# Longformer attention with an FFN: weight decode moved from the prelude into the first FFN group

## The chip, the cores and the metric

The kernel runs on one core of one Trainium2 chip. The metric is device time in microseconds (us) of one execution. Before the change it is 1021.1 us, the median of 3 runs (1018.6 to 1021.68).

## What is computed

The inputs are queries, keys and values of 8 batches x 8 heads: 512 local tokens and 32 global ones, 64 wide. Local tokens attend to the global ones and to local ones within 32 positions; global tokens attend to all. The result goes through a feed-forward network (FFN) with weights of 512 x 2048 and 2048 x 512. All of it is float32.

```python
def _attn_ref(q_l, k_l, v_l, q_g, k_g, v_g):
    ...
    s_g = scale * np.matmul(q_g, k_all.transpose(0, 1, 3, 2))
    out_g = np.matmul(sm(s_g), v_all)
    s_ll = scale * np.matmul(q_l, k_l.transpose(0, 1, 3, 2))
    mask = np.abs(pos[:, None] - pos[None, :]) <= window
    s_ll = np.where(mask, s_ll, -1000000000.0)
    ...
    out_l = np.matmul(a_l, np.concatenate([v_g, v_l], axis=2))

def _moe_ref(x, w_in, w_out, alpha):
    h = x @ w_in
    g = np.maximum(h, 0.0) + alpha * np.minimum(h, 0.0)
    return (g @ w_out).astype(np.float32)
```

The weights reach the kernel as the bits of float64 numbers, so it has to decode them into float32 before it can use them.

## The kernel before

**Units.** The main loop counts t from -19 (NPRE is 19); u = t + 19 is the unit. Units 0 to 18 are the *prelude*: attention only, because the FFN needs the attention of a whole batch first. From unit 19 on, every unit also does one step of the FFN.

**Attention** goes by pairs of heads: 32 pairs P, four to a batch, four units to a pair (unit 4P + s). In a unit, `local_scores` takes a quarter of a pair's scores (PE), adds the mask (VectorE, L243) and exponentiates (ScalarE, L247); `softmax_tail` normalizes (L208, L209, L214). Once per pair, `global_softmax` starts with a row maximum on VectorE (L270), in unit 4P + 2; it serves below as a mark of how far attention has come. The transposes and the product with the values of pair P come in units 4P + 2 to 4P + 6.

**FFN** goes by groups: eight groups of 512 local tokens (one batch each), and one of 256 global tokens. A group has 16 steps f, one per unit. `f1` multiplies the attention's result, split in two float32r halves `xh` and `xl` by `split_x` (L386, L387), with the f-th block of w_in, 12 matmuls into `h_ps`; VectorE applies the activation (L404, L405), ScalarE and GpSimd split the result into `gh` (L407) and `gl` (L408). `f2`, two units later (LAG), adds 12 matmuls into the group's outputs `o`. So the first group is units 19 to 34, and L404 marks the units in the trace. The next group can start when the four pairs of its batch are through.

**Weight decode.** The weights are 32 pieces of 512 KB, piece 2f of w_in and 2f + 1 of w_out. A piece is loaded on SP's queue (`load_weights`, L104). `decode_words` takes two ScalarE operations (L112, L113), three of VectorE (L114, L116, L117) and an add on GpSimd (L119). One unit later `split_weights` takes one of ScalarE (L125) and a subtraction on GpSimd (L126). After that the piece stays in SBUF for the rest of the kernel. f1 of step f needs piece 2f, from unit 19 + f on; f2 needs piece 2f + 1, from unit 21 + f on.

**What sets the order.** `weights_step(u)` stands at the end of each unit. RATE says how many pieces it decodes: the first tuple, by u modulo its length, in the prelude, the second from unit 19 on. With `((1, 1, 0), (2, 1))` the prelude's units decode 13 pieces, and units 19 to 31 the other 19: two in even units, one in odd ones. Each decode of piece i also issues the load of piece i + 6; the first six loads are issued ahead of the loop, right behind the first load of queries and keys (`load_pair(0)`).

The order within each engine's queue is made when the program is built: a planner goes by program order as priority and by a simulated time, so that work whose inputs are there may be put ahead of earlier work that waits. From unit 4 on the attention has a priority of 50 places ahead (HP, HPU). From unit 36 (PIN) PE's matmuls keep program order. Working tiles share pools: the tag "st" has 18 buffers (NST), for `xh`, `xl`, `g`, `gh`, `gl`, the values `vx`, and the `t` and `r` of decode; the tag "w" has 33 (NWB), for raw and for decoded weights.

In units 0 to 17 `keep_warm` adds four matmuls on zeros to each unit.

Of the kernel before, what the change touches and what calls it, by code (L numbers as in the profile page):

```python
# [44 lines left out]
GS = (2, "mid")  # L45
EV = dict(pt0=(2, "mid"), pt1=(4, "pre"), ptg=(4, "pre"), pv0=(5, "mid"), pv1=(6, "mid"))
SM = (2, "post")
RATE = ((1, 1, 0), (2, 1))
GROUPS = [("l", b) for b in range(NB)] + [("g", 0)]


# [8 lines left out]
def longformer_ffn(ctx: ExitStack, tc: tile.TileContext, qk, qkr, gn, vt, vx, w, alpha, out):  # L60
# [41 lines left out]
    def load_weights(f, j):  # L102
        wraw[f, j] = wpool.tile([128, 1024], U32, tag="w", name="wraw")
        nc.sync.dma_start(wraw[f, j], w[f, j].bitcast(U32))  # L104
# [3 lines left out]
    def decode_words(f, j):  # L108
        words = wraw.pop((f, j)).rearrange("p (n two) -> p n two", two=2)
        low, high = words[:, :, 0], words[:, :, 1]  # L110
        t, r = stage("wt"), stage("wr", I32)
        nc.scalar.activation(t, high.bitcast(F32), AF.Abs)  # L112
        nc.scalar.activation(r, low, AF.Copy, scale=2.0**-29)  # L113
        nc.vector.tensor_scalar(t, t, CLAMP_LO, CLAMP_HI, op0=ALU.max, op1=ALU.min)  # L114
        tu = t.bitcast(U32)
        nc.vector.tensor_scalar(tu, tu, 3, 0x3FFFFFFF, op0=ALU.logical_shift_left, op1=ALU.bitwise_and)  # L116
        nc.vector.scalar_tensor_tensor(tu, high, 0xC0000000, tu, op0=ALU.bitwise_and, op1=ALU.bitwise_or)  # L117
        ti = t.bitcast(I32)
        nc.gpsimd.tensor_tensor(ti, ti, r, op=ALU.add)  # L119
        wmid[f, j] = t  # L120

    def split_weights(f, j):
        t = wmid.pop((f, j))
        wt = wpool.tile([128, 2, 512], F32R, tag="w", name="wt")
        nc.scalar.copy(wt[:, 0, :], t)  # L125
        nc.gpsimd.tensor_tensor(wt[:, 1, :], t, wt[:, 0, :].bitcast(F32), op=ALU.subtract)  # L126
        wts[f, j] = wt
# [50 lines left out]
    def load_pair(P):  # L178
        hi[P] = work.tile([128, NQ + NKR], F32, tag="hi", name="qk_raw", bufs=2)
        nc.sync.dma_start(hi[P], qkr[P])  # L180
# [348 lines left out]
    pieces = [(f, j) for f in range(NF) for j in range(2)]  # L529
    ahead = 6  # L530
    state = [0]

    def weights_step(u):
        k = state[0]
        n = RATE[0][u % len(RATE[0])] if u < NPRE else RATE[1][u % len(RATE[1])]
        new = [i for i in range(k, min(k + n, len(pieces)))]
        for i in new:
            if i + ahead < len(pieces):
                load_weights(*pieces[i + ahead])
            decode_words(*pieces[i])  # L540
        state[0] += len(new)
        done.append([pieces[i] for i in new])
        if len(done) > 1:
            for key in done.pop(0):
                split_weights(*key)
# [4 lines left out]
        return tc.high_priority(offset=HP) if u >= HPU else nullcontext()  # L550

    load_pair(0)
    for k in range(ahead):
        load_weights(*pieces[k])
    NT = len(GROUPS) * NF
    for t in range(-NPRE, NT + LAG):
        u = t + NPRE
        pinned[0] = u >= PIN
        if u < NWARM:
            keep_warm(WARM[0])  # L560
        with boost(u):
            attn_pre(u)
        G, f = divmod(t + 1, NF)
        last = 0 <= t + 1 < NT and f == 0
        if 0 <= t < NT:
            f1(t)
        if last:
            for c in range(NC - 1):
                split_x(G, c)
        with boost(u):  # L570
            attn_mid(u)
        if last:
            split_x(G, NC - 1)
        if t >= LAG:
            f2(t - LAG, 0)
        if u < NWARM:
            keep_warm(WARM[1])
        with boost(u):
            attn_post(u)
        if t >= LAG:  # L580
            f2(t - LAG, 1)
        weights_step(u)
# [74 lines left out]
```

## Time and profile before

| | |
|---|---|
| median of 3 runs | 1021.1 us |
| the profiled execution | 1017.19 us, its span 1015.4 us |
| PE busy | 984.7 us, 97% of the span |
| VectorE (DVE) busy | 659.9 us, 65% |
| ScalarE (ACT) busy | 507.4 us, 50% |
| GpSimd (POOL) busy | 407.7 us, 40% |
| DMA | 133.01 MB, 131 GB/s on the mean |
| first L404 (start of the FFN) | 95.96 us |
| L404 of the second group's first step | 231.69 us |
| last add of a decode (L119) | 201.58 us |

The profile is of one execution; times in it count from the start of its span. An instruction has a line of the kernel, an engine, the tile that it writes and those that it reads. Matmuls are pipelined, so a PE that is shown busy need not be at its peak. A row in square brackets after an instruction tells how long its engine was idle before it, and what it waited for. The chain of waits is followed back from the last instruction: at each step to what released it.

### The profile page before, as it was taken

The numbers are of one execution on the slowest core, as the hardware profiler recorded it, in microseconds if no ns is written. First come the engines' busy times: TensorE is split into PE (matmuls) and PEld (weight loads), VectorE is DVE, ScalarE is ACT, GpSimd is POOL, SyncE is SP. The second block draws the span as 40 slices with busy tenths as digits, with TensorE's granted clock in tenths as the row PEclk, the third lists the DMA queues.
The fourth block names the chain that finished last, engine by engine and source line by source line (L and its number), as shares of the span: only waits on it lengthen the run. The fifth ranks groups of instructions, "written<-read, shape, count | busy, mean of one in ns | idle before, by whom it ended". The sixth has DMA issues, their size and how long they took to land.

```text
span 1015.4 us, 17227 instructions
## 1 busy us (share of the span) xinstructions
PE 984.7 (97%) x5592; PEld 790.2 (78%) x5592; DVE 659.9 (65%) x2274; ACT 507.4 (50%) x1347; POOL 407.7 (40%) x330
## 2 busy tenths in 40 slices
PE   7798989998999999999999999999999999999998
PEld 4455767776888888888888888888888888888798
DVE  8978778776666766676767666766667665322322
ACT  6667566575445555455446555654555542211121
POOL 7611567653344344334344344433443432222222
PEclk9987999999999999999999999999999999999999
DMA  9545432145444554455455554455455532100010
GB/s 349 224 141 176 140 116 68 60 123 185 147 138 133 177 158 137 141 167 169 135 152 158 171 153 143 144 179 157 118 149 178 159 107 79 42 1 1 1 43 22
DMA packets 95275, 133.01 MB, mean 131 GB/s; under 512 B 10192, under 2 KB 53712, under 8 KB 95184
## 3 DMA queue, kind: packets, MB, share of 16 engines
q1 hardware_dynamic: 95184, 131.91, 41.5%
q8 instruction: 44, 0.72, 0.3%
q14 instruction: 47, 0.39, 0.1%
HBM read 100.93 MB, written 30.93 MB: 130 GB/s over the span
## 4 chain that ended last, share of the span: by engine, by line
PE 84%; DVE 9%; ACT 2%; issue 2%; DMA 1%; POOL 0%; SPq 0%; DVEq 0%; ACTq 0%; POOLq 0%
PE o L92 35%; PE h_ps L92 35%; PE o_ps L92 5%; PE s_ps L92 5%; PE g_ps L92 3%; DVE wt L114 1%; DVE wt L117 1%; DVE pt_sb L318 1%; DVE p_sb L243 1%; PE warm L92 1%; ACT p_sb L214 1%; DVE g L404 1%; DVE wt L116 1%; DVE g L405 1%; ACT p_sb L247 0%
## 5 line engine op out<-in xcount | busy, mean ns | idle before, releaser
L92 PE MATMUL h_ps<-xh,wt 128*128 128x512 f32 (+1 forms) x1152 | 351.8, 389 | 2.8 <-DVE g L405 2.8
L408 POOL TENSOR_TENSOR gl<-g,gh 128x512 fp32r<-128x512 f32 (+1 forms) x144 | 177.5, 1233 | 418.1 <-ACT gh L407 382.6
L92 PE MATMUL o<-gh,wt 128*128 128x512 f32 (+1 forms) x1152 | 282.5, 386 | 1.5 <-ACT ost L302 1.5
L92 PEld LDWEIGHTS o<-gh,wt 128*128 128x128 f32 x1152 | 205.8, 188 | 48.5 <-ACT ost L302 2.5
L92 PEld LDWEIGHTS h_ps<-xh,wt 128*128 128x128 f32 x1152 | 207.4, 191 | 43.4 <-DVE g L405 3.3
L92 PE MATMUL h_ps<-xl,wt 128*128 128x512 f32 (+1 forms) x576 | 222.4, 387 | 0.9 <-DVE xl L387 0.9
L407 ACT CAST gh<-g 128x512 fp32r<-128x512 f32 (+1 forms) x144 | 86.1, 598 | 260.9 <-DVE g L405 241.4
L404 DVE TENSOR_SCALAR g<-h_ps,alpha_sb 128x512 f32<-128x512 f32 (+1 forms) x144 | 103.3, 717 | 125.3 <-PE h_ps L92 123.0
L214 ACT ACTIVATE p_sb<-p_sb,rz 128x192 f32<-128x192 f32 (+1 forms) x252 | 102.3, 454 | 118.1 <-DVE rz L209 115.8
L92 PE MATMUL o<-gl,wt 128*128 128x512 f32 (+1 forms) x576 | 151.4, 383 | 0.0
L247 ACT ACTIVATE p_sb<-p_sb,mn 128x224 f32<-128x224 f32 (+2 forms) x256 | 115.8, 454 | 39.5 <-DVE mn L243 39.3
L92 PEld LDWEIGHTS h_ps<-xl,wt 128*128 128x128 f32 x576 | 109.4, 190 | 25.2 <-DVE xl L387 1.1
L92 PEld LDWEIGHTS o<-gl,wt 128*128 128x128 f32 x576 | 104.5, 188 | 23.9 <-issue 0.8
L208 DVE TENSOR_SCALAR rz<-z 128x1 f32<-128x1 f32 x256 | 38.3, 151 | 97.4 <-ACT p_sb L247 96.0
L297 DVE STREAM_TRANSPOSE pt_sb<-sg_sb 32x64 f32<-32x64 f32 x384 | 90.6, 236 | 10.6 <-ACT sg_sb L280 4.9
L192 POOL TENSOR_TENSOR hi<-rawq,hi 64x512 fp32r<-64x512 f32 x48 | 62.1, 1294 | 88.0 <-DMA vt<-in_vt_dram 50.1
L405 DVE SCALAR_TENSOR_TENSOR g<-h_ps,g 128x512 f32<-128x512 f32 (+1 forms) x144 | 94.1, 653 | 2.8
L195 POOL TENSOR_TENSOR kl<-rawk,hi 128x640 fp32r<-128x640 f32 x48 | 75.9, 1582 | 3.8
L119 POOL TENSOR_TENSOR wt<-wt,wr 128x512 int32<-128x512 int32 x32 | 42.4, 1324 | 77.2 <-DVE rz L208 40.2
L243 DVE CUSTOM_DVE_ANT_0 p_sb<-s_ps,mask 128x192 f32<-128x192 f32 x192 | 64.3, 364 | 13.5 <-PE s_ps L92 11.9
L92 PE MATMUL o_ps<-pt_sb,vt 128*64 128x160 f32 (+4 forms) x832 | 68.2, 288 | 3.6 <-ACT pt_sb L302 1.7
L92 PEld LDWEIGHTS o_ps<-pt_sb,vt 128*64 128x64 f32 (+2 forms) x832 | 48.7, 135 | 21.9 <-issue 11.9
(85 smaller groups left out, 1043.7 us busy)
## 6 DMA issues: line engine op xcount, KB each, us to landing
scratch<-p_sb SPq DMA_DIRECT2D x192, 112.0 KB, 2.4
wraw<-in_w_dram SPq DMA_DIRECT2D x32, 512.0 KB, 6.7
vt<-in_vt_dram SPq DMA_DIRECT2D x32, 512.0 KB, 4.9
rawk<-in_qk_dram SPq DMA_DIRECT2D x96, 160.0 KB, 2.9
rawq<-in_qk_dram SPq DMA_DIRECT2D x96, 128.0 KB, 2.7
pt_sb<-scratch SPq DMA_DIRECT2D x48, 256.0 KB, 2.8
gn<-in_gn_dram SPq DMA_DIRECT2D x32, 304.0 KB, 5.3
pt_sb<-scratch SPq DMA_DIRECT2D x48, 192.0 KB, 2.9
```

The costliest lines, as they stand in the source:

```text
L92: ins = nc.tensor.matmul(*a, **k)
L119: nc.gpsimd.tensor_tensor(ti, ti, r, op=ALU.add)
L192: nc.gpsimd.tensor_tensor(q, raw[64:128], q.bitcast(F32), op=ALU.subtract)
L195: nc.gpsimd.tensor_tensor(kl[P, h], raw, t.bitcast(F32), op=ALU.subtract)
L214: nc.scalar.activation(r, r, AF.Copy, scale=rz[:parts, e : e + 1])
L243: nc.vector.tensor_tensor_reduce(out=pr, in0=s[:, 256 * e : 256 * e + nn], in1=masks[e], scale=-0.125, scalar=3.0e38, op0=ALU.add, op1=ALU ...
L247: nc.scalar.activation(pr, pr, AF.Exp, bias=mn[:, e : e + 1], scale=-1.0, accum_out=z[:, e : e + 1])
L297: nc.vector.transpose(dst, src)
L404: nc.vector.tensor_scalar(g[:, 0:n], h[:, 0:n], 0.0, alpha_sb[:, f : f + 1], op0=ALU.min, op1=ALU.mult)
L405: nc.vector.scalar_tensor_tensor(g[:, 0:n], h[:, 0:n], 0.0, g[:, 0:n], op0=ALU.max, op1=ALU.add)
L407: nc.scalar.copy(gh[:, 0:n], g[:, 0:n])
L408: nc.gpsimd.tensor_tensor(gl[:, 0:n], g[:, 0:n], gh[:, 0:n].bitcast(F32), op=ALU.subtract)
```

## The change

RATE becomes `((0, 0, 1), (2,))`. In the prelude one piece is decoded in every third unit (2, 5, 8, 11, 14, 17): six pieces in place of 13. Units 19 to 31 decode two pieces each: 26 in place of 19. In both kernels the last piece is in unit 31. The first six loads are no longer issued ahead of the loop, but one at the end of each of the units 0 to 5, behind the attention's loads of these units.

```diff
-RATE = ((1, 1, 0), (2, 1))
+RATE = ((0, 0, 1), (2,))
...
     def weights_step(u):
+        if u < ahead:
+            load_weights(*pieces[u])
         k = state[0]
...
     load_pair(0)
-    for k in range(ahead):
-        load_weights(*pieces[k])
     NT = len(GROUPS) * NF
```

## The prediction

> **What bounds the kernel now.** I read the windows view first, cut where the kernel changes its work: 20 to 60 us (attention with weight decode), 60 to 86 us (attention alone), 104 to 200 us (first FFN group, attention and decode), and 200 to 232 us (the end of that group). Columns: stretch, length, then busy time of PE, PEld, DVE, ACT and POOL.
>
> ```profile
> 20.00:60.00 40.00, 32.41 (x171) 20.17 (x170) 34.29 (x105) 24.70 (x68) 26.23 (x20) 0.87 0.63 239
> 60.00:86.00 26.00, 24.39 (x241) 15.63 (x239) 20.63 (x117) 20.53 (x72) 0.00 (x0) 1.00 0.39 124
> 104.00:200.00 96.00, 91.73 (x547) 68.67 (x548) 77.20 (x207) 59.92 (x145) 62.01 (x48) 0.96 0.30 101
> 200.00:232.00 32.00, 30.82 (x176) 24.36 (x175) 24.23 (x93) 20.35 (x56) 15.68 (x13) 0.95 0.38 111
> ```
>
> Two things are to be seen. GpSimd does nothing at all from 60 to 86 us, so decode sits in two blocks with a hole between them: one early in the prelude, one in the first FFN group. And in the second block no engine has much to spare: PE 91.7 of 96 us, VectorE 77.2, GpSimd 62.0. Next I read the chain of waits (start, length, what), to see which of them leads.
>
> ```profile
> 95.96 0.75 DVE g L404
> ...
> 97.49 5.49 PE h_ps L92 x12
> ...
> 110.98 1.55 DVE wt L117
> 112.62 1.28 POOL wt L119
> 113.92 0.70 ACT wt L112
> ...
> 192.20 2.80 PE h_ps L92 x12
> ```
>
> Around 110 us the chain walks through one piece of decode on three engines (L117, L119, L112); at 192 us it is plain matmuls. So the first FFN group is bound by decode in its first part and by PE in its last. The FFN starts at 95.96 us (unit 19, the first L404).
>
> **What the prelude gains.** Of 13 pieces in the prelude's units, 6 stay. What a piece costs there is read from the spacing of the pairs, by the row maximum L270, once per pair (pairs 0, 1, 2 and 4):
>
> ```profile
> 20.77 0.44 DVE L270 TENSOR_REDUCE gm<-g_ps 128x1 f32<-128x288 f32 x1
> 40.88 0.45 DVE L270 TENSOR_REDUCE gm<-g_ps 128x1 f32<-128x288 f32 x1
> 59.64 0.46 DVE L270 TENSOR_REDUCE gm<-g_ps 128x1 f32<-128x288 f32 x1 [1.48 <-PE g_ps L92]
> 86.12 0.46 DVE L270 TENSOR_REDUCE gm<-g_ps 128x1 f32<-128x288 f32 x1 [0.82 <-PE g_ps L92]
> ```
>
> From pair 0 to pair 2 take 38.9 us, with eight pieces of decode among them; from pair 2 to pair 4 take 26.5 us with none. A piece costs the prelude (38.9 - 26.5) / 8 = 1.55 us. When are they decoded?
>
> ```profile
> 43.77 0.67 ACT L112 ACTIVATE wt<-wraw 128x512 f32<-128x512 f32 x1
> ...
> 88.96 0.62 ACT L386 CAST xh<-x_raw 128x512 fp32r<-128x512 f32 x1
> 89.96 0.68 ACT L112 ACTIVATE wt<-wraw 128x512 f32<-128x512 f32 x1
> ...
> 97.47 0.62 ACT L407 CAST gh<-g 128x512 fp32r<-128x512 f32 x1 [1.11 <-DVE g L405]
> 97.99 0.68 ACT L112 ACTIVATE wt<-wraw 128x512 f32<-128x512 f32 x1
> ```
>
> L112 opens a piece. The twelfth starts at 43.77 us, far ahead of its unit 16. The thirteenth (unit 18) waits until 89.96, just behind the last `xh` of split_x, which stands ahead of it in the program; the fourteenth (unit 19) follows the first `gh`. I infer that buffers of the tag "st" are handed out in program order: decode can run ahead until it meets a split_x or f1 that still waits for its input. So in the changed kernel the six pieces of units 2 to 17 will be done by some 30 us, and the other 26 can't use the hole, since their turn comes behind split_x (unit 18) and f1 (unit 19). Six pieces leave the early block: 6 x 1.55 = 9.3 us. PE limits that: it is busy 32.4 of the 40 us from 20 to 60, keep_warm included, so those pairs can lose at most 7.6 us. With 0.7 us for the thirteenth piece, which runs beside the first f1, I take 8.3 us (bounds 4 and 11), and the FFN starts at 95.96 - 8.3 = 87.7 us.
>
> **The loads.** Six weight loads that stood ahead of gn and the second qk_raw on SP now stand behind them (the issue as it is before; then the row of the waits: total, times, longest):
>
> ```profile
> 1.65 3.02 SPq L104 DMA_DIRECT2D wraw<-in_w_dram x6
> ACT wt L112 <- DMA wraw<-in_w_dram: 4.4, 1, 4.4
> ```
>
> gn and qk_raw of pair 1 are issued up to 3 us earlier, but no engine is shown waiting for either. The one wait for a weight (4.4 us, ScalarE's first piece) is in front of no exponential, and the first decode moves from unit 0 to unit 2, behind its load. I cost this at nothing; what hides it is attention's own chain from the first qk_raw. Without that cover it is 3 us at most, either way. Later loads are issued six pieces, three units, ahead of their decode, and no other wait for a weight is shown.
>
> **What the first FFN group pays.** Units 19 to 31 decode 19 pieces before, 26 after. A piece by its rows (busy and mean from the groups of lines, 104 to 200 us; then min/median/max over all 32 pieces):
>
> ```profile
> L126 POOL TENSOR_TENSOR wt<-wt 128x512 fp32r<-128x512 f32 x18 | 23.4, 1305 | 8.6 <-ACT wt L125 4.3 <-issue 3.9
> L119 POOL TENSOR_TENSOR wt<-wt,wr 128x512 int32<-128x512 int32 x17 | 22.1, 1299 | 23.8 <-DVE wt L117 12.4 <-PE o L92 2.6 <-DVE gz L277 2.2
> L408 POOL TENSOR_TENSOR gl<-g,gh 128x512 fp32r<-128x512 f32 x11 | 14.2, 1294 | 0.7 <-ACT gh L407 0.4
> L114 DVE TENSOR_SCALAR wt<-wt x32: 398/472/1304, 7.1 to 199.1; 128x512 f32<-128x512 f32 x32
> L116 DVE TENSOR_SCALAR wt<-wt x32: 405/428/1431, 8.2 to 199.8; 128x512 uint32<-128x512 uint32 x32
> L117 DVE SCALAR_TENSOR_TENSOR wt<-wraw,wt x32: 676/693/1790, 9.3 to 200.8; 128x512 uint32<-128x512 uint32 x32
> ```
>
> GpSimd: 1.30 + 1.31 = 2.60 us. VectorE: 0.40 + 0.41 + 0.68 = 1.48 us at the least, but up to three times that. Why they stretch:
>
> ```profile
> 109.90 0.42 DVE L116 TENSOR_SCALAR wt<-wt 128x512 uint32<-128x512 uint32 x1
> 110.89 1.64 DVE L117 SCALAR_TENSOR_TENSOR wt<-wraw,wt 128x512 uint32<-128x512 uint32 x1
> 110.68 1.31 POOL L126 TENSOR_TENSOR wt<-wt 128x512 fp32r<-128x512 f32 x1 [2.09 <-ACT wt L125]
> ```
>
> L116 with GpSimd idle takes its 0.42 us. L117 meets GpSimd's L126 (110.68 to 111.99) and ends at 112.53, 0.54 us behind it, having taken 1.64 instead of 0.69. So the two engines' parts of a piece run one after the other: 2.60 + 1.48 = 4.08 us of a path both use. The FFN's own `gl` (1.29 us a unit) goes over it too, and 62.0 - 23.4 - 22.1 - 14.2 = 2.3 us of other GpSimd work.
>
> The 13 units, from L404 to L404, take 200.09 - 95.96 = 104.1 us (rows below). The last piece's add, at 201.58, lies just behind that point, so 18 pieces count: 18 x 4.08 + 13 x 1.29 + 2.5 = 92.7 us of the shared path, 89% of the time. After: I let two pieces trail, so 24 x 4.08 + 16.8 + 2.5 = 117.2 us. If the path is never free, the stretch grows by 117.2 - 104.1 = 13.1 us; if it stays free 11% of the time, by 27.6; I take 15, near the floor, because more decode in the queues leaves fewer gaps.
>
> [...]
>
> What the trace shows of more decode per unit bounds it otherwise. Units alternate two pieces (even) and one (odd); L404 of units 29 to 32, and the last piece's add on GpSimd:
>
> ```profile
> 176.61 0.74 DVE L404 TENSOR_SCALAR g<-h_ps,alpha_sb 128x512 f32<-128x512 f32 x1
> 182.94 0.74 DVE L404 TENSOR_SCALAR g<-h_ps,alpha_sb 128x512 f32<-128x512 f32 x1
> 193.83 0.75 DVE L404 TENSOR_SCALAR g<-h_ps,alpha_sb 128x512 f32<-128x512 f32 x1
> 200.09 0.75 DVE L404 TENSOR_SCALAR g<-h_ps,alpha_sb 128x512 f32<-128x512 f32 x1
> 201.58 1.29 POOL L119 TENSOR_TENSOR wt<-wt,wr 128x512 int32<-128x512 int32 x1 [2.56 <-DVE wt L117]
> ```
>
> Unit 29 (one piece) takes 6.3 us, unit 30 (two) 10.9, unit 31 (one) 6.3: 4.6 us for the extra piece, though part is given back in the next unit. Seven more at 4.6 would be 32 us, the upper bound; zero is the lower, if PE's 91.7 us hid them all. There is no room behind the stretch: from 200 to 232 us PE is busy 30.8 of 32.
>
> **A wait that is added.** With two pieces in every unit, two `t` tiles of the unit before stay in "st" (18 buffers) until split_weights has run, and f1's g, gh and gl need their turn behind them. The next gh on ScalarE, and the attention's exponentials queued behind it, would then wait for GpSimd's L126 (1.3 us). That is inside the 15 us as long as L126 isn't late; once a unit it would be 13 x 1.3 = 17 us, within the upper bound.
>
> **The sum.** -8.3 + 0 + 15 = +6.7 us. Against the profiled execution of 1017.2 us (span 1015.4) that is 1023.9; that execution lies 3.9 us under the median shown, 1021.1, so I forecast 1021.1 + 6.7 = 1027.8 us.
>
> **Rivals.** *The cover holds (faster).* PE sets the pace in the later part of the group already (the chain at 192 us), and its queue takes up the two-piece units in between: the odd units ran at 6.3 us. If VectorE's operations fit between GpSimd's, and decode trails by one unit more without an f1 missing its weight, the group pays 2 us and the kernel gains 8.3 - 2 = 6.3: 1015. It decides when a two-piece unit takes less than 104.1 / 13 + 8.3 / 13 = 8.6 us from L404 to L404. For it: PE near full; against it: 10.9 us for unit 30. Chance 0.25. *The terms cancel*: about 8 us each way, 1021; chance 0.12. *Decode uses the hole*: "st" doesn't hold it, and pieces of units 19 and up are decoded from 50 to 86 us; then four fewer in the group, 1021 - 6 = 1015; against it, nothing moved there before. Chance 0.04. *The clock drops (slower still).* The twelve matmuls at 97.49 took 5.49 us where those at 192.20 took 2.80. If gaps in PE bring the slow pace back for four such groups in the FFN, 4 x 2.7 = 11 us come on top: 1039. Chance 0.09.
>
> [...]
>
> **The numbers.** My forecast has 0.50. About 3 us (0.3%) is what a measurement of this kernel can tell from no change. Faster: 0.25 + 0.04 = 0.29; same: 0.12; slower: 0.50 + 0.09 = 0.59. The forecast's own range is 1021.1 + 1.8 to + 19, from a prelude gain of 11 or 4 and a cost of 13 or 23. The whole range reaches down through the cover rival to 1013 and up to the edge of the clock rival, 1040.
>
> **What would show it.** Right: six L119 before 40 us and none until the FFN starts; L270 of pair 4 near 78 us instead of 86.1; first L404 near 88; unit 32's L404 near 88 + 119 = 207; two-piece units of 9 us and more, with L114 to L117 of 1.2 us and up more often; the second group's first L404 near 238 instead of 231.7. Wrong: units 20 to 31 at 8.6 us or less; L119 between 50 and 86 us; a first L404 later than 92; or PE pausing for a DMA.

## The result, and the profile after

The changed kernel takes 1026.0 us (median of 14 runs, 1022.6 to 1027.86), the kernel before 1018.12 us (14 runs, 1012.67 to 1021.68). The ratio is 1.0077 [1.0059, 1.0095]: 7.9 us slower. The profiled execution of the changed kernel took 1026.16 us, its span 1024.3. Ratios, here and below, leave out single executions that took far longer than the rest, such as the profiled one of e1 (1354.65 us, at a mean clock of 0.656).

The windows view of the changed kernel, over the same four stretches as before the change (the last three columns are granted PE clock, share of the DMA engines and GB/s):

```profile
20.00:60.00 40.00, 39.87 (x263) 24.99 (x264) 31.86 (x138) 27.15 (x88) 12.91 (x11) 1.00 0.64 234
60.00:86.00 26.00, 26.00 (x208) 16.94 (x205) 14.22 (x80) 14.95 (x50) 0.00 (x0) 1.00 0.33 106
104.00:200.00 96.00, 87.10 (x458) 63.62 (x456) 88.92 (x207) 64.02 (x152) 73.29 (x55) 0.89 0.36 122
200.00:232.00 32.00, 25.20 (x132) 19.03 (x130) 27.10 (x79) 17.52 (x46) 21.07 (x18) 0.83 0.40 114
```

Two things have turned round. From 20 to 86 us PE is now full (39.87 of 40, then 26.00 of 26), with the clock at 1.00; before, it had gaps and 0.87. From 104 to 200 us PE has less to do than before (87.1 instead of 91.7 us), while VectorE went from 77.2 to 88.9 us and GpSimd from 62.0 to 73.3.

Next the marks in the timeline of the changed kernel (start, length): L270 of pairs 0, 1, 4 and 9, and L404 of unit 19 (the FFN's first), unit 32 and the second group's first unit, 35:

```profile
10.70 0.45 DVE L270 TENSOR_REDUCE gm<-g_ps 128x1 f32<-128x288 f32 x1
25.62 0.45 DVE L270 TENSOR_REDUCE gm<-g_ps 128x1 f32<-128x288 f32 x1
75.17 0.46 DVE L270 TENSOR_REDUCE gm<-g_ps 128x1 f32<-128x288 f32 x1 [2.96 <-PE g_ps L92]
85.58 0.75 DVE L404 TENSOR_SCALAR g<-h_ps,alpha_sb 128x512 f32<-128x512 f32 x1
209.61 0.73 DVE L404 TENSOR_SCALAR g<-h_ps,alpha_sb 128x512 f32<-128x512 f32 x1
240.97 0.75 DVE L404 TENSOR_SCALAR g<-h_ps,alpha_sb 128x512 f32<-128x512 f32 x1 [5.32 <-PE h_ps L92]
257.13 0.45 DVE L270 TENSOR_REDUCE gm<-g_ps 128x1 f32<-128x288 f32 x1
```

Of the kernel before, only pair 9's mark is still needed:

```profile
248.41 0.46 DVE L270 TENSOR_REDUCE gm<-g_ps 128x1 f32<-128x288 f32 x1
```

Pair 9 (unit 38) serves as an end mark: from it to the end of the span take 767.0 us before (1015.4 - 248.41) and 767.2 after (1024.3 - 257.13). So the whole difference lies ahead of it, and it splits into three:

| | before | after | difference |
|---|---|---|---|
| start of the FFN (first L404) | 95.96 | 85.58 | -10.4 |
| 13 units, L404 of unit 19 to that of unit 32 | 104.1 | 124.0 | +19.9 |
| unit 32 to the end mark | 48.3 | 47.5 | -0.8 |
| end mark | 248.41 | 257.13 | +8.7 |

The windows view cut at these points tells what PE did in each part. First before, then after:

```profile
0.00:95.96 95.96, 80.18 (x533) 50.41 (x534) 78.07 (x302) 66.94 (x195) 42.50 (x50) 0.91 0.62 225
95.96:200.09 104.13, 99.26 (x572) 73.92 (x571) 82.74 (x219) 64.27 (x155) 66.79 (x52) 0.93 0.30 102
200.09:248.41 48.32, 43.48 (x257) 34.22 (x257) 33.94 (x121) 30.69 (x82) 23.36 (x19) 0.96 0.46 138
```

```profile
0.00:85.58 85.58, 80.30 (x531) 50.13 (x532) 59.34 (x278) 53.94 (x171) 23.91 (x36) 1.00 0.61 218
85.58:209.61 124.03, 112.63 (x629) 82.69 (x628) 113.29 (x271) 82.33 (x200) 89.33 (x67) 0.90 0.33 115
209.61:257.13 47.52, 40.20 (x202) 31.03 (x201) 30.14 (x94) 23.81 (x60) 22.56 (x18) 0.86 0.43 126
```

Read the matmul counts: 533 + 572 + 257 = 1362 and 531 + 629 + 202 = 1362. (A matmul that lies across a cut is counted on both sides of it; uncut they are 1359 and 1358.) The work up to the mark is the same; the longer 13 units took 57 more matmuls of it, since attention ran ahead of the FFN, and 55 fewer were left behind unit 32. So the 13 units must not be judged alone: what is not done in them comes later. Note also that PE is shown busy for 233.1 us in place of 222.9 for those 1362 matmuls, while its idle time hardly changes (25.5 us before, 24.0 after). Why the same matmuls were shown busy for 10 us more, these rows do not tell.

The groups of the changed kernel from 104 to 200 us (busy, mean ns, idle before):

```profile
L119 POOL TENSOR_TENSOR wt<-wt,wr 128x512 int32<-128x512 int32 x21 | 27.9, 1328 | 18.6 <-DVE wt L117 9.3 <-DVE rz L208 3.5 <-DVE rz L209 2.2
L126 POOL TENSOR_TENSOR wt<-wt 128x512 fp32r<-128x512 f32 x19 | 27.4, 1447 | 4.4 <-ACT wt L125 4.3
L408 POOL TENSOR_TENSOR gl<-g,gh 128x512 fp32r<-128x512 f32 x10 | 14.5, 1452 | 0.6 <-POOL wt L119 0.6
...
L117 DVE SCALAR_TENSOR_TENSOR wt<-wraw,wt 128x512 uint32<-128x512 uint32 x20 | 19.5, 976 | 0.2
L116 DVE TENSOR_SCALAR wt<-wt 128x512 uint32<-128x512 uint32 x20 | 19.3, 967 | 0.3
L114 DVE TENSOR_SCALAR wt<-wt 128x512 f32<-128x512 f32 x20 | 17.1, 857 | 3.0 <-ACT wt L112 2.9
```

VectorE's three in the same stretch before the change:

```profile
L116 DVE TENSOR_SCALAR wt<-wt 128x512 uint32<-128x512 uint32 x18 | 14.8, 825 | 0.3
L117 DVE SCALAR_TENSOR_TENSOR wt<-wraw,wt 128x512 uint32<-128x512 uint32 x17 | 14.8, 873 | 0.2
...
L114 DVE TENSOR_SCALAR wt<-wt 128x512 f32<-128x512 f32 x18 | 12.6, 697 | 8.6 <-ACT wt L112 8.3 <-issue 0.2
```

Both sides stretch. VectorE's three operations, 1.48 us a piece at the least, took 2.40 us on the mean before and take 2.80 now; GpSimd's L126 went from 1305 to 1447 ns and its `gl` from 1294 to 1452.

Last, the prelude. The sixth and seventh adds of a decode in the timeline, and four rows of the chain of waits from 30 to 77 us, where all the work on the chain is PE's:

```profile
36.38 1.28 POOL L119 TENSOR_TENSOR wt<-wt,wr 128x512 int32<-128x512 int32 x1 [4.35 <-DVE xgt L357]
94.22 1.29 POOL L119 TENSOR_TENSOR wt<-wt,wr 128x512 int32<-128x512 int32 x1 [3.22 <-DVE mn L243]
```

```profile
31.27 2.82 PE o_ps L92 x24
34.09 2.43 PE warm L92 x5
...
41.49 1.54 PE warm L92 x5
...
46.98 3.73 PE o_ps L92 x43
```

Six pieces are decoded before 40 us and none until the FFN has begun. With less decode, the matmuls of `keep_warm` come to stand on the chain: they are 39.0% of it from 30 to 77 us, where they were 6.7% from 30 to 90 us before the change.

### The profile page after: what moved, and what is told of

It reads as the page before. It is cut to its first block, busy times and chain, and to the rows that moved or that the text cites. A ratio compares the mean times of both kernels' runs of the same rounds, so it can differ in the third digit from the quotient of the medians.

```text
span 1024.3 us, 17228 instructions
## 1 busy us (share of the span) xinstructions
PE 995.2 (97%) x5592; PEld 795.7 (78%) x5592; DVE 668.1 (65%) x2274; ACT 504.8 (49%) x1347; POOL 411.0 (40%) x330
## 4 chain that ended last, share of the span: by engine, by line
PE 83%; DVE 10%; issue 2%; ACT 2%; DMA 1%; POOL 1%; DVEq 0%; ACTq 0%; POOLq 0%; SPq 0%
PE o L92 34%; PE h_ps L92 34%; PE o_ps L92 6%; PE s_ps L92 5%; PE g_ps L92 3%; DVE wt L117 2%; DVE wt L114 2%; PE warm L92 2%; DVE wt L116 1%; DVE g L404 1%; DVE g L405 1%; DMA wraw<-in_w_dram 1%; DVE p_sb L243 1%; DVE pt_sb L318 1%; ACT p_sb L247 0%
## 5 line engine op out<-in xcount | busy, mean ns | idle before, releaser
L92 PE MATMUL o<-gh,wt 128*128 128x512 f32 (+1 forms) x1152 | 289.9, 394 | 1.6 <-ACT gh L407 1.1
L92 PEld LDWEIGHTS o<-gh,wt 128*128 128x128 f32 x1152 | 210.6, 192 | 50.9 <-ACT gh L407 2.9
L404 DVE TENSOR_SCALAR g<-h_ps,alpha_sb 128x512 f32<-128x512 f32 (+1 forms) x144 | 103.2, 717 | 129.9 <-PE h_ps L92 128.8
L297 DVE STREAM_TRANSPOSE pt_sb<-sg_sb 32x64 f32<-32x64 f32 x384 | 90.7, 236 | 10.6 <-ACT sg_sb L280 4.9
L405 DVE SCALAR_TENSOR_TENSOR g<-h_ps,g 128x512 f32<-128x512 f32 (+1 forms) x144 | 94.1, 654 | 2.9
L192 POOL TENSOR_TENSOR hi<-rawq,hi 64x512 fp32r<-64x512 f32 x48 | 62.2, 1296 | 79.9 <-DMA vt<-in_vt_dram 53.4
L92 PE MATMUL o_ps<-pt_sb,vt 128*64 128x160 f32 (+4 forms) x832 | 72.0, 296 | 0.9 <-DVE x_glb L354 0.5
L119 POOL TENSOR_TENSOR wt<-wt,wr 128x512 int32<-128x512 int32 x32 | 42.3, 1322 | 38.0 <-DVE wt L117 11.5
```

The source lines that it names most:

```text
L92: ins = nc.tensor.matmul(*a, **k)
L192: nc.gpsimd.tensor_tensor(q, raw[64:128], q.bitcast(F32), op=ALU.subtract)
L297: nc.vector.transpose(dst, src)
L404: nc.vector.tensor_scalar(g[:, 0:n], h[:, 0:n], 0.0, alpha_sb[:, f : f + 1], op0=ALU.min, op1=ALU.mult)
L405: nc.vector.scalar_tensor_tensor(g[:, 0:n], h[:, 0:n], 0.0, g[:, 0:n], op0=ALU.max, op1=ALU.add)
```

## The experiments

One table holds what the traces gave, so that each experiment below needs only its point. "Behind" is unit 32 to the end mark, with the matmuls in it. From the end mark to the end of the span each of these kernels takes 767.0 to 767.7 us, and the matmuls up to it add up to 1359 to 1362 (1325 or 1326 where `keep_warm` is halved).

| kernel | time to before [95%] | first L404 | 13 units | behind | end mark |
|---|---|---|---|---|---|
| before | 1 | 95.96 | 104.1 | 48.3 (257) | 248.41 |
| after | 1.0077 [1.0059, 1.0095] | 85.58 | 124.0 | 47.5 (202) | 257.13 |
| e1 loads alone | 0.9978 [0.9960, 0.9996] | | | | |
| e11 loads alone, again | 0.9972 [0.9951, 0.9994] | 93.02 | 97.9 | 53.4 (271) | 244.27 |
| e2 RATE alone | 1.0157 [1.0125, 1.0189] | 90.66 | 122.6 | 44.8 (207) | 258.09 |
| e9 six loads at unit 0 | 1.0204 [1.0183, 1.0225] | 98.80 | 123.7 | 47.0 (203) | 269.46 |
| e7 13 pieces in the group | 1.0075 [1.0050, 1.0099] | 107.59 | 90.9 | 55.7 (308) | 254.20 |
| e3 after, L126 on VectorE | 1.0010 [0.9995, 1.0026] | 84.92 | 117.8 | 45.8 (243) | 248.53 |
| e4 before, L126 on VectorE | 1.0047 [1.0025, 1.0069] | 97.79 | 97.8 | 55.3 (290) | 250.89 |
| e8 after, no L119 | 0.9874 [0.9861, 0.9887] | 80.54 | 97.0 | 57.6 (294) | 235.19 |
| e5 after, r in the raw words | 1.0037 [1.0024, 1.0050] | 82.50 | 118.4 | 49.2 (248) | 250.10 |
| e10 loads alone, r in the raw words | 1.0115 [1.0093, 1.0137] | 99.14 | 103.1 | 57.6 (279) | 259.87 |
| e6 after, half of keep_warm | 1.0025 [1.0012, 1.0038] | 77.81 | 122.8 | 46.3 (207) | 246.84 |
| e12 e3 + e5 + e6 | 1.0055 [1.0034, 1.0076] | 81.31 | 112.4 | 58.4 (310) | 252.14 |

e1 and e11 are the same kernel; the trace that is used is e11's.

### The two parts alone: e1 and e11, e2

The loads alone, which is the changed kernel with the old RATE:

```diff
-RATE = ((0, 0, 1), (2,))
+RATE = ((1, 1, 0), (2, 1))
```

> RATE as before, only the six first weight loads spread over units 0 to 5. My theory (the loads are hidden by attention's own start): within 3 us of before, ratio 0.997 to 1.003. Rival (the loads' new place delays the first decode or the later loads): 1.004 or more, and a wait for a weight load on ScalarE.

> The kernel of e1 once more, for a trace at the usual clock: time 0.996 to 1.000 of before, first row maximum near 11 us in place of 20.8; if the loads alone move the FFN's start, first L404 near 91 us, if the decode of 13 pieces holds it, near 96.

The RATE alone, with the loads ahead of the loop as before:

```diff
-RATE = ((1, 1, 0), (2, 1))
+RATE = ((0, 0, 1), (2,))
```

> RATE as after, the six loads ahead of the loop as before. My theory (all of the loss comes from RATE): 1.006 to 1.010 of before, units 20 to 31 at some 9.5 us each, first L404 near 86 us. Rival (the loads' new place makes part of it): 1.004 or less.

The loads alone gain 0.2 to 0.3%, twice on different chips. From e11's timeline, L404 of units 19 and 32:

```profile
93.02 0.74 DVE L404 TENSOR_SCALAR g<-h_ps,alpha_sb 128x512 f32<-128x512 f32 x1
190.87 0.75 DVE L404 TENSOR_SCALAR g<-h_ps,alpha_sb 128x512 f32<-128x512 f32 x1 [1.87 <-POOL wt L126]
```

The RATE alone costs 1.57% (16 us by the ratio), more than both theories expected; so the loads give back 8 us under the new RATE and only 2 to 3 under the old. In the trace the FFN starts 2.9 us earlier by the loads alone (93.02), 5.3 by the RATE alone (90.66), and 10.4 by both: half of the earlier start belongs to the loads. Its windows view from 60 to 90 us shows the prelude without them:

```profile
60.00:90.00 30.00, 26.63 (x207) 17.03 (x208) 21.49 (x114) 20.33 (x70) 0.00 (x0) 0.79 0.42 138
```

The clock there is 0.79, where the changed kernel has 1.00. e2's six runs lie between 1026.8 and 1037.5 us, and the profiled one (1027.07) is among its fastest, so the trace holds only 10 of the 16 us.

### Behind the attention's loads, or spread: e9

All six loads at the end of unit 0, so behind `gn` and the second `qk_raw`, but not spread:

```diff
-        if u < ahead:
-            load_weights(*pieces[u])
+        if u == 0:
+            for k in range(ahead):
+                load_weights(*pieces[k])
```

> RATE as after, the six first loads all at the end of unit 0, behind gn of pair 0 and qk_raw of pair 1, but not spread. If what the loads' new place brings is that gn and qk_raw go first: the first global scores near 9 us as in after (16.6 with the loads ahead), time 1.005 to 1.010 of before. Rival (spreading over six units matters in itself): 1.012 to 1.018, as with the loads ahead of the loop.

It is the slowest kernel of all, above both expectations: spreading counts, and more than expected. The edit moves only the six loads, but the planner orders the other queues anew with them, and the time holds both. SP's queue in the changed kernel, then in e9 (start, length of the issue):

```profile
2.59 0.93 SPq L104 DMA_DIRECT2D wraw<-in_w_dram  x2
3.56 0.52 SPq L172 DMA_DIRECT2D vt<-in_vt_dram  x1
```

```profile
2.59 3.25 SPq L104 DMA_DIRECT2D wraw<-in_w_dram  x6
6.31 0.33 SPq L172 DMA_DIRECT2D vt<-in_vt_dram  x1
```

The first pair's mark is at 10.68 in e9 and 10.70 in the changed kernel: getting `gn` and `qk_raw` first is worth the same. From there e9 falls behind. Its values `vt` stand behind six loads, but that is not what holds it: their first matmul starts at 32.05, and the wait that ends there is for L304 on VectorE. What stands ahead there is decode. The sixth L112 starts at 19.83 us in e9, at 29.73 in the changed kernel. Here are VectorE's timeline up to pair 1's mark, the row of PE's waits for it (total, times, longest; the longest ends at 32.05), and ten microseconds of the windows:

```profile
22.83 1.50 DVE L114 TENSOR_SCALAR wt<-wt 128x512 f32<-128x512 f32 x1
24.25 1.76 DVE L117 SCALAR_TENSOR_TENSOR wt<-wraw,wt 128x512 uint32<-128x512 uint32 x1
...
26.00 1.46 DVE L116 TENSOR_SCALAR wt<-wt 128x512 uint32<-128x512 uint32 x1
...
27.49 1.63 DVE L117 SCALAR_TENSOR_TENSOR wt<-wraw,wt 128x512 uint32<-128x512 uint32 x1
...
30.56 0.45 DVE L270 TENSOR_REDUCE gm<-g_ps 128x1 f32<-128x288 f32 x1
```

```profile
PE o_ps L92 <- DVE pt_sb L304: 5.7, 2, 4.9
```

```profile
40.00:50.00 10.00, 10.00 (x52) 5.78 (x50) 4.30 (x23) 4.86 (x16) 0.00 (x0) 0.50 0.36 115
```

The copy that PE waited for (L304) stands behind these four operations of decode. Pair 1 comes 4.9 us later than in the changed kernel (25.62); PE is idle for 4.9 us up to 32.05, and from 32 to 54 us its granted clock is 0.50 (0.60, 0.50 and 0.70 in the windows of ten microseconds from 30, 40 and 50 us on, 1.00 on either side). The FFN starts 13.2 us later, and the end mark is 12.3 us later. In between nothing differs: the 13 units take 123.7 us with this start and 124.0 with the other. That is true of every kernel with the new RATE whose decode is untouched (122.6 to 124.0): in these runs the cost of the first group did not depend on the prelude.

What holds the clock at 0.50 is not shown: in the row from 40 to 50 us PE is busy throughout (10.00 of 10.00) at that clock.

### How many pieces: e7

One piece in every unit, 19 in the prelude and 13 in the group, with the new loads:

```diff
-RATE = ((0, 0, 1), (2,))
+RATE = ((1,), (1,))
```

> RATE ((1,), (1,)): 19 pieces in the prelude, one in each of units 19 to 31. If a piece's price is what counts (some 1.5 us in the prelude, 2.7 us in the first group at 26 pieces, little below what PE covers): first L404 near 105 us, units of the group at 7.3 us, set by PE; the six pieces moved from the group save less than they cost: 0.998 to 1.006 of before. Rival (price in the group stays 2.7 us down to one piece per unit): the group saves 16 us and the time is 0.990 to 0.995.

Both edges in its timeline:

```profile
107.59 0.74 DVE L404 TENSOR_SCALAR g<-h_ps,alpha_sb 128x512 f32<-128x512 f32 x1
198.53 0.75 DVE L404 TENSOR_SCALAR g<-h_ps,alpha_sb 128x512 f32<-128x512 f32 x1
```

The units are fast, 7.0 us each, but the FFN starts too late, and the time misses its expectation (0.998 to 1.006) by a little. With the new loads there are now three points. In the prelude, 6, 13 and 19 pieces start the FFN at 85.58, 93.02 and 107.59 us: 1.06 us for each of the first seven, 2.4 for each of the next six. In the group, 13, 19 and 26 pieces take 90.9, 97.9 and 124.0 us: 1.2 and then 3.7 us each. Both curves bend, and about 13 in the prelude is the best of the three. With the part behind unit 32 counted in, so that each kernel has 827 to 831 matmuls, the group's three points are 146.6, 151.3 and 171.6 us: 0.8 and then 2.9 us a piece.

### What in the group costs: e3, e4, e8

L126, the second of the two GpSimd operations of a piece, on VectorE; on the changed kernel (e3) and on the one before (e4):

```diff
-nc.gpsimd.tensor_tensor(wt[:, 1, :], t, wt[:, 0, :].bitcast(F32), op=ALU.subtract)
+nc.vector.tensor_tensor(wt[:, 1, :], t, wt[:, 0, :].bitcast(F32), op=ALU.subtract)
```

> After, with the subtraction L126 on VectorE in place of GpSimd. If the two engines' shared path sets the unit (1.30 us of GpSimd out, 0.69 us of VectorE in, 0.61 us less of the path per piece): a two-piece unit falls from 9.5 to about 8.3 us, 13 units by some 15 us, the time to 0.985 to 0.995 of before. Rival (VectorE's own work sets the unit): 0.69 us more for each of 26 pieces, 10 us or more slower than after, 1.015 or more of before.

> Before, with L126 on VectorE. Shared path: less to gain than in after, since units of 1.5 pieces are near what PE needs: 0.990 to 0.997 of before, and the gap between the two RATEs closes. Rival (VectorE's own work): 19 x 0.69 = 13 us more in the first group, 1.008 or more.

And with L119 left out besides, so that decode has nothing on GpSimd (e8):

```diff
-nc.gpsimd.tensor_tensor(ti, ti, r, op=ALU.add)
```

> After, with L126 on VectorE and the add L119 left out, so the weights lack their low part; GpSimd then does nothing for decode. Shared path: a two-piece unit falls to what PE or VectorE's own time needs, 7.3 to 8.3 us, and VectorE's L114 to L117 go back to 0.40, 0.42 and 0.69 us but where gl runs; time 0.985 to 0.993 of before. Rival (latency from engine to engine, or ScalarE's share): units stay above 9 us, time 1.000 or more.

The windows of e3 and e4 from 104 to 200 us, and of e8 from 104 to 178:

```profile
104.00:200.00 96.00, 82.57 (x457) 59.53 (x457) 93.09 (x223) 65.41 (x149) 52.32 (x37) 0.96 0.35 118
```

```profile
104.00:200.00 96.00, 94.19 (x558) 69.88 (x558) 84.82 (x217) 59.75 (x140) 45.67 (x34) 1.00 0.25 82
```

```profile
104.00:178.00 74.00, 70.76 (x394) 52.98 (x393) 72.20 (x187) 54.66 (x128) 18.75 (x12) 0.98 0.37 126
```

And e3's two groups of the same operations as above:

```profile
L116 DVE TENSOR_SCALAR wt<-wt 128x512 uint32<-128x512 uint32 x21 | 13.4, 643 | 0.1
L114 DVE TENSOR_SCALAR wt<-wt 128x512 f32<-128x512 f32 x20 | 11.2, 562 | 1.2 <-ACT wt L112 1.1
```

With less on GpSimd, VectorE's own operations shorten although VectorE got more of them: L114 from 857 to 562 ns, L116 from 967 to 643. The 13 units fall by 6.2 us, and the kernel by 6.8 (ratio 1.0010 in place of 1.0077). Had VectorE's count of operations been the bound, e3 would have been slower than the changed kernel. But the 15 us off that the shared path alone would have given did not come. VectorE is by then shown busy for 93.09 of 96 us, with operations that are still longer than alone (L116 643 ns, 405 at the least). e8 takes the other GpSimd operation away as well, and the 13 units go to 97.0 us, 7.5 each, with all 26 pieces in them; the ratio of 0.9874 lies where it was expected. So the two engines' turn-taking is what the group pays for in the main (124.0 us with both of GpSimd's operations of a piece, 117.8 with one, 97.0 with none), and VectorE's own work looks like the next limit close behind (72.20 of 74 us in e8). Both edits also shorten a piece's way from engine to engine; what that alone is worth, these runs do not separate.

On the kernel before, the same edit did not pay (e4, between its two expectations): its units fall by 6.3 us too, but 33 more matmuls are left for the part behind (290 against 257), which grows by 7.0, and the start is 1.8 us later. There PE was busy for 94.19 of 96 us.

### The added wait, and keep_warm: e5, e10, e6, e12

`r` written over raw words that are no longer needed, so that it takes no buffer of the tag "st"; on the changed kernel (e5), and on the loads alone (e10, with the old RATE):

```diff
-        t, r = stage("wt"), stage("wr", I32)
+        t, r = stage("wt"), low.bitcast(I32)
```

> After, with r written over the low words of the raw weights in place of a tile of its own: one buffer of the tag st less for each piece in work. Shared path of VectorE and GpSimd as the cause: no change beyond 3 us against after (1.005 to 1.010 of before), perhaps slower, since GpSimd then reads r with a stride. Rival (the 18 buffers hold f1 and decode back in two-piece units): 8 us or more gained, 1.000 of before or less, and fewer waits of ScalarE's L112 and L407 on GpSimd.

> RATE as before, the loads spread as in after, r over the raw words. If the 18 buffers also press with 1.5 pieces per unit: 2 to 5 us less than with the loads alone, 0.993 to 0.996 of before. Rival (they press only with two pieces in every unit): 0.997 to 1.000.

e5 gains 4 us, between the two theories. Its 13 units take 5.6 us less than the changed kernel's, with the same 24 adds in them, although VectorE's three operations got longer (L114 969, L116 1020, L117 1060 ns). The adds, which read `r` with a stride there, took 1.315 us at the median, 1.293 in the changed kernel. e10 loses 14 us against the loads alone, where no theory expected a loss, and it loses in every part (start +6.1, units +5.3, behind +4.2). The edit moves whole queues, since the planner orders by a simulated time that depends on buffers. What the buffers themselves cost stays open.

Half of the matmuls of `keep_warm`, on the changed kernel (e6):

```diff
-WARM = (2, 2)
+WARM = (1, 1)
```

> After, with half of the matmuls on zeros in the prelude (36 in place of 72). In after's trace PE is never idle from 40 to 85 us, and 47 of these matmuls lie in 40 to 80 us. If PE now sets the prelude: 36 fewer at 0.23 us, first L404 4 to 8 us earlier (78 to 82), the time 0.999 to 1.004 of before. Rival (they keep PE's clock up, or PE only fills its gaps with them): first L404 at 85 us or later, time as after or slower, 1.007 or more.

The FFN starts 7.8 us earlier (77.81), and the kernel gains 5.3 us by the ratio. PE's granted clock up to that point is 0.96, in the changed kernel 1.00. As expected, PE with its warm-up matmuls sets the changed prelude.

The three edits that had each helped the changed kernel, together (e12):

```diff
-WARM = (2, 2)
+WARM = (1, 1)
...
-        t, r = stage("wt"), stage("wr", I32)
+        t, r = stage("wt"), low.bitcast(I32)
...
-nc.gpsimd.tensor_tensor(wt[:, 1, :], t, wt[:, 0, :].bitcast(F32), op=ALU.subtract)
+nc.vector.tensor_tensor(wt[:, 1, :], t, wt[:, 0, :].bitcast(F32), op=ALU.subtract)
```

> After with three changes that each took time off it: L126 on VectorE (6.8 us), r over the raw words (4 us), half of keep_warm (5.3 us). If they act on different waits: 1010 to 1013 us on a before of 1016.6, ratio 0.993 to 0.997. Rival (the first two free the same path, or what is won is lost again before unit 38): 0.998 to 1.003.

They do not add up: 1.0055. Its last window, from unit 32 to the end mark:

```profile
193.73:252.14 58.41, 50.92 (x310) 38.59 (x311) 40.38 (x149) 34.81 (x94) 24.14 (x20) 0.94 0.44 128
```

Its 13 units are short (112.4 us), but 310 matmuls are left behind them, where the changed kernel has 202, and that part takes 58.4 us. Over all kernels this part is 44.8 to 49.2 us with 202 to 257 matmuls in it, and 53.4 to 58.4 with 271 to 310. That is where short units lose part of their gain: they end before attention's share of the matmuls is done.

## Why the prediction was right, and where it was not

**Direction and size.** The net was +6.7 us against a measured +7.9, and the forecast's base, 1021.1, was 3 us above the later median. The terms were less good than their sum: -8.3 + 0 + 15 was predicted, -10.4 + 19.9 - 0.8 happened. That the sum came out within 2 us is in part luck, since the errors had opposite signs.

**"Six pieces ... done by some 30 us, and the other 26 can't use the hole."** Right but for the time: the sixth add starts at 36.38, the seventh at 94.22. That decode waits for its turn behind split_x and f1 is in the order of the trace; that the buffers are the reason was inferred and is still not shown, as e5 and e10 go opposite ways.

**The prelude's gain, 8.3 us.** PE as the cap was the right kind of limit, and e6 shows it. But the gain was 5.3 us for the RATE alone and 10.4 with the loads, so neither is the 8.3; that it lies between them is luck. The price of 1.55 us a piece held roughly and on the mean only: under the new loads the first seven pieces cost 1.06, the next six 2.4.

**The loads, "I cost this at nothing".** This is the step that failed. The prediction looked for an engine shown waiting for `gn`, `qk_raw` or a weight, found none, and bounded the term at 3 us. The loads were worth 5.1 us of the start under the new RATE, and e9 against the changed kernel shows 13.2 us between two positions of the same six loads. What the wait rows did not show stands in the queues. In the kernel before, `gn` landed at 13.6 us (issued at 4.72, 8.9 us to landing) while PE was kept busy by `keep_warm`; its matmuls started at 15.99, and pair 0's mark came at 20.77, behind three operations of decode on VectorE of 1.38, 1.65 and 1.30 us. With the loads behind `gn` the mark comes at 10.70. In e2 all six L112 of the prelude have started by 17.36 us, in the changed kernel by 29.73: where the loads stand early, decode stands ahead of attention. How the 5.1 us divide between that and the clock of e2's prelude (0.79 from 60 to 90 us) is not shown.

**The first group, 15 us.** The mechanism held: e3 and e8 take GpSimd's operations away, VectorE's shorten, and the units with them. The term was too small, and the step is the occupancy. The 24 adds that were counted did end inside the stretch (those at 209.52 and 215.78 did not), so the path is about the 117.2 us of the prediction; other GpSimd work was nearer 5 us than the 2.5 counted. I chose 15, that is 117.2 of 119.1 us or 98% busy, "because more decode in the queues leaves fewer gaps". It came to 117.2 of 124.0, 94.5%, about half way between the 89% of before and full. That is no limit of the path: e5 has the same 24 adds in 118.4 us, which is 99%, and near the 119.1 us of the forecast. What fills the gaps in e5, the freed buffers or the new order, stays open.

The 13.1 us that a path which is never free would have added were passed by 6.8 us, and the mean durations of both engines grew together (VectorE's three from 2.40 to 2.80 us a piece, L126 from 1305 to 1447 ns). That the engines take turns shows in single operations. From 96 to 200 us of the kernel before, nine L116 had no operation of GpSimd beside them and took 0.41 to 0.43 us; nine of the other ten took 0.79 to 1.43 us and ended 0.28 or 0.29 us behind one of GpSimd's (the tenth, 0.43 us, had begun first). `gl` counts among these operations too: the L114 at 114.64 us took 0.77 us and ended 0.28 us behind it.

**The added wait.** It is not seen. In the 13 units of the changed kernel ScalarE's `gh` is shown waiting 11.9 us for L405 on VectorE, and neither it nor an exponential for L126.

**No room behind the stretch.** Right for the net (31.6 us before and 31.4 after from unit 32's L404 to the second group's first), but for another reason than PE's 30.8 of 32 us: between these two marks PE was busy for 24.48 of 31.36 us afterwards, with 106 matmuls where it had 175, since attention had run ahead, and at a clock of 0.78.

**The rivals.** The cover does not hold: 9.54 us a unit on the mean (5.5 to 12.2), where 8.6 was the limit. The terms do not cancel, and the hole is not used. The two paces that the prediction compares went with two clocks, 0.50 from 97.49 to 102.98 us and 1.00 from 192.20 to 195.00; that gaps in PE bring the slow one is not shown. The clock did drop in the group, from 0.96 to 0.89 (104 to 200 us) and from 0.95 to 0.83 (200 to 232), which is 0.07 x 96 + 0.12 x 32 = 10.6 us of full clock; but it rose in the prelude, so that the mean up to the end mark is 0.93 in both kernels, and the 11 us did not come on top of the sum. Nor does the clock set the 13 units. In e2, the RATE alone, they run at the 0.93 of the kernel before and take 122.6 us in place of 104.1; in e9, at 0.94, they take 123.7:

```profile
90.66:213.29 122.63, 110.27 (x624) 79.32 (x622) 108.99 (x266) 82.31 (x200) 90.59 (x67) 0.93 0.32 111
```

**The checks.** Pair 4 at 75.17 (78 predicted), first L404 at 85.58 (88), unit 32 at 209.61 (207), the second group at 240.97 (238): each within 3 us.

**The best version.** Spreading the loads without touching the RATE (e1, e11) beats both kernels, by 0.2 to 0.3% against the one before and 1.0% against the changed one. It can be told from no change only just.

**What stays open.** Why e2's other runs are up to 10 us slower than its profiled one; what the "st" buffers cost; what in e5 closed the gaps of the path; and how e9's 13 us divide between decode that stands ahead of attention and the low clock, of which the trace shows the order and not the shares.

## What to carry to other kernels

Price work that is moved between stages by what the receiving stage shares: here operations of two engines took turns (an L116 of 0.42 us took up to 1.43 beside one of GpSimd's in the kernel before), and the last seven pieces cost 3.7 us each in the group where the six before them cost 1.2 (2.9 and 0.8 with what was left behind). Don't price the order of loads by the wait rows alone; here loads for which no costly wait was shown moved the start of the FFN by 5.1 and by 13.2 us, and the work behind them stood in another order. Cut both traces at marks that the change can't move, and count the matmuls in each cut, before a short stage is called a gain.

## What was not expected of the hardware

The clock of PE in the prelude differed with the order of six loads: 1.00 throughout in the changed kernel, 0.79 from 60 to 90 us with the loads ahead of the loop, 0.50 from 40 to 50 us with all six in unit 0, at nearly the same number of matmuls up to the FFN (530 to 531).

GpSimd's operations stretched too: its 128x512 subtraction grew from 1305 to 1447 ns and its `gl` from 1294 to 1452 as VectorE went from 77.2 to 88.9 us busy of 96.

Small edits that leave the arithmetic alone moved the time by up to 14 us (e5 by -4, e10 by +14 with the same edit), while the 767 us behind unit 38 stayed the same to within 0.7 us in all kernels.
